# RMS weights folded into the up weights, a fixed token scale and a tanh read from PSUM in the last stage of an attention, mixture-of-experts and feed-forward kernel

## Chip, core and metric

The kernel runs on one core of one Trainium2 chip. The metric is the device time of one execution in microseconds (us). Matmuls run on TensorE (PE, with its weight loads PEld), elementwise work on VectorE (DVE), ScalarE (ACT) and GpSimd (POOL). Transfers are issued from the queues of SyncE (SP), ACT and POOL.

## The reference, cut to what matters

An attention with gates gives `x` of 3072 tokens by 320. A router sends each token to one of 8 experts (320 to 1024 to 320). The last stage, which the change is about, works on the result:

```
rms = sqrt(mean(x * x, axis=-1) + 1e-6)
xn  = x / rms * rms_g                      # rms_g: 320 weights
g   = xn @ w_gate                          # 320 x 1536
silu = g * (1 / (1 + exp(-g)))
out = (silu * (xn @ w_val)) @ w_out        # 1536 x 320
```

The weights arrive as float64. The kernel makes float32 of them on DVE (five integer steps, "narrowing") and then a pair of float16 values, high and rest. A product is three or so float16 matmuls: high by high, rest by high, high by rest.

## The kernel before

**Order.** The order on each engine and each queue is written out by hand. An engine takes its instructions strictly in that order. A DMA queue issues in order too, and an instruction that waits holds up all behind it. `route` sorts the tokens, `moe` runs the experts block by block, `moe_tail` ends it, and `ffn` is the last stage.

**Expert stage.** `moe` has a loop over 28 blocks `j` of 128 tokens. `gather(j)` fetches rows on POOL's queue, `xpose(j)` turns them on SP's queue into a tile `xt` (two buffers, so `xpose(2)` has to wait for the matmuls of `up(0)`), `up(j)` multiplies, and `down(j)`, two blocks later, multiplies with `W2A` and `W2B`. At its start POOL also has to finish two slices of `W2B` (L883, L884), behind `gather(2)` and `gather(3)`. `tick()` (L1160) works in the background on one weight job of the last stage: a load on SP, the five narrowing steps on DVE (L1265 to L1269), and a step that scales by `WSC` on ACT (L1290), takes the rest on DVE (L1296) and stores through POOL's queue. There are 24 jobs for the up weights (`UWS`) and four for the down weights (`DWS`), which come last. At blocks 23 to 26 (`FJ`) the first 512 tokens of the last stage are fetched, normalised and split (`fetch`, `norm1` to `norm4`).

**Last stage.** Six groups `n` of 512 tokens, each with 12 blocks `f` of 128 hidden units. `upf(n, f)` (L1492) does eight matmuls of 512 columns for the gate into the PSUM tile `pg` and eight for the value into `pv`. Both have one tag with four buffers, so block `f` writes over what block `f-2` held. Behind the matmuls: a product with `kvec` on DVE (L1502, it undoes the scale of each token), tanh on ACT (L1503), two products on DVE (`u`, L1510 and L1511), the float16 high part on ACT (L1516), the rest on POOL (L1517). `downf` of group `n-1` runs inside group `n`, behind block 9 (`DF`): four times 36 matmuls of 320 columns, an ACT copy with a scale for each token, and a scatter from POOL.

**Token scale.** `norm1` makes 1/rms, `norm2` multiplies by it and by the weights `G`, `peak` and `norm3` take a power of two for each token out of its largest value, `norm4` splits into float16, and `spread` and `undo` turn the inverse powers into the tile `kvec`, by four small matmuls (L1434) a group. For group 1 this runs beside group 0 (`beside`), from group 2 on inside `downf` (`stage`, with `DS`).

**Down weights.** Of 12 tiles, four come back from `DWS` and the other eight (`LJ`) are narrowed inside `upf`, by `wjob`: `more(1)` stands ahead of L1510 and another behind L1517, so two of the 40 narrowing steps go to a block, and the job's `rest` on POOL (L1486) frees the buffer for the next load `wload`. All of that has to be over before `downf(0)`.

Of the kernel before, what the change touches and what calls it, by code (L numbers as in the profile page):

```python
# [37 lines left out]
FJ = (23, 24, 25, 26)  # L38
LJ = 8
DF = 9  # L40
NS = (6, 8)
TS = ((0, 7),), ((1, 1), (2, 3), (3, 5))
DS = ((0, 1), (2,), (3, 4, 5, 6), (7,))
# [18 lines left out]
XSC = 2.0**-8  # L62
ORDER = (
# [12 lines left out]
class Net:  # L76
# [38 lines left out]
    def consts(self):  # L115
# [14 lines left out]
        self.NH = cp.tile([128, 4], F32, name="NH")  # L130
        self.zero = cp.tile([128, YC // 3], F32, name="zero3")
# [15 lines left out]
        self.DWS = dp.tile([NF, 128, 2 * DM], F16, name="DWS")  # L147
# [939 lines left out]
    def moe(self):  # L1087
# [70 lines left out]
        slot = [0]  # L1158

# [12 lines left out]
        for j in range(NJ):  # L1172
# [35 lines left out]
            if j == FJ[0]:  # L1208
                self.fetch(0, first=True)
            elif j == FJ[1]:  # L1210
                self.norm1(0)
                self.tokens(0)
            elif j == FJ[2]:
                for m in range(4):
                    self.norm2(0, m)
                self.norm3(0)
            elif j == FJ[3]:
                for m in range(4):
                    self.norm4(0, m)
# [52 lines left out]
    def ffn_jobs(self):  # L1272
        nc = self.nc
        jobs = []

        def job(src, n, fin):
            st = {}

            def load(t):
                t = st["t"] = t.bitcast(I32)  # L1280
                nc.sync.dma_start(t[:, 0 : 2 * n], src.bitcast(I32))

            def s1():
                st["v"], steps = self.narrow(st["t"], n)
                for step in steps:
                    step()

            def s2():
                of = st["t"][:, 0:320].bitcast(F16)
                nc.scalar.activation(of[:, 0:n], st["v"], AF.Copy, scale=WSC)  # L1290
                fin(st["v"], of, st["t"])

            return load, s1, s2

        def rest(out, v, hi):
            nc.vector.scalar_tensor_tensor(out=out, in0=v, scalar=WSC, in1=hi, op0=ALU.mult, op1=ALU.subtract)  # L1296

        def up(f, g):
            def fin(v, of, t):
                rest(of[:, 384:640], v[:, 0:256], of[:, 0:256])  # L1300
                rest(of[64:128, 256:384], v[64:128, 256:384], of[64:128, 256:384])
                nc.gpsimd.dma_start(self.UWS[f, :, g], of)  # L1302

            return job(self.i["wu"][f, g], 384, fin)

        def down(f):
            def fin(v, of, t):
                rest(of[:, DM : 2 * DM], v, of[:, 0:DM])
                nc.gpsimd.dma_start(self.DWS[f], of)

            return job(self.i["wo"][128 * f : 128 * f + 128], DM, fin)

        for f in range(NF):
            jobs += [up(f, 0), up(f, 1)]
        for f in range(NF - LJ):
            jobs.append(down(f))
        return jobs

    def fetch(self, n, first=False):
# [3 lines left out]
        for m in range(4):  # L1323
            i = 4 * n + m
            if first:
# [4 lines left out]
                if m == 3:  # L1330
                    self.G = t[:, DX : DX + DM]
                    u = self.stg()
                    self.idh0 = t[:, 3 * DX : 3 * DX + 64].bitcast(F16)
                    nc.gpsimd.tensor_copy(self.idh0, self.id)
                    X["xr"] = [
                        a.bitcast(F16).rearrange("p (s c) -> p s c", s=2)
                        for a in (t[:, 2 * DX : 3 * DX], u[:, 0:DX], u[:, DX : 2 * DX], u[:, 2 * DX : 3 * DX])
                    ]
                    nc.sync.dma_start(self.G, self.i["rg"].partition_broadcast(128))
# [8 lines left out]
    def norm1(self, n):  # L1348
# [5 lines left out]
        nc.vector.tensor_scalar(s[:, 1], s[:, 0], 1.0 / DM, 1e-6, ALU.mult, ALU.add)  # L1354
# [9 lines left out]
    def norm2(self, n, m, pool=False):  # L1364
        nc, X = self.nc, self.X[n]
        x, rs = X["yg"][m][:, 0:DM], X["rs"][:, m : m + 1]
        if pool:
            nc.scalar.activation(x, x, AF.Copy, scale=rs)  # L1368
            nc.gpsimd.tensor_tensor(x, x, self.G, ALU.mult)
            return  # L1370
        nc.vector.scalar_tensor_tensor(out=x, in0=x, scalar=rs, in1=self.G, op0=ALU.mult, op1=ALU.mult)
        self.peak(n, m)

    def peak(self, n, m):
        nc, X = self.nc, self.X[n]
        x = X["yg"][m][:, 0:DM]
        nc.vector.tensor_reduce(X["s"][:, 0, m : m + 1], x, AX.X, ALU.max, apply_absolute_value=True)  # L1377

    def norm3(self, n):

        nc, X = self.nc, self.X[n]
        mx, sc, ik, os = (X["s"][:, k] for k in (0, 3, 4, 5))
        mi = mx.bitcast(I32)
        nc.vector.tensor_scalar(mi, mi, 0x7F800000, None, ALU.bitwise_and)
        nc.vector.scalar_tensor_tensor(
            out=sc.bitcast(I32), in0=mi, scalar=float(27 << 23), in1=self.kmax.to_broadcast([128, 4]),
            op0=ALU.max, op1=ALU.subtract, reverse1=True,
        )
        nc.vector.tensor_scalar(ik.bitcast(I32), mi, float(27 << 23), float(-(1 << 23)), ALU.max, ALU.add)
        nc.vector.scalar_tensor_tensor(out=os, in0=ik, scalar=0.5 / WSC, in1=ik, op0=ALU.mult, op1=ALU.mult)  # L1390
        X["sc"], X["ik"], X["os"] = sc, ik, os

    def spread(self, n):
        nc, X = self.nc, self.X[n]
        X["ib"] = self.F.tile([128, 4, 128], BF, tag="ib", bufs=1, name="ib")
        nc.gpsimd.tensor_scalar(
            X["ib"], X["ik"].unsqueeze(2).to_broadcast([128, 4, 128]), 1.0 / WSC, 0.0, ALU.mult, ALU.add
        )

    def norm4(self, n, m, pool=False):  # L1400
        nc, X = self.nc, self.X[n]
        x, sc = X["yg"][m][:, 0:DM], X["sc"][:, m : m + 1]
# [3 lines left out]
        nc.scalar.activation(xr[:, 0, 0:DM], x, AF.Copy, scale=sc)  # L1406
        if pool:
            nc.scalar.activation(x, x, AF.Copy, scale=sc)
            nc.gpsimd.tensor_tensor(xr[:, 1, 0:DM], x, xr[:, 0, 0:DM], ALU.subtract)
        else:  # L1410
            nc.vector.scalar_tensor_tensor(
                out=xr[:, 1, 0:DM], in0=x, scalar=sc, in1=xr[:, 0, 0:DM], op0=ALU.mult, op1=ALU.subtract
# [16 lines left out]
    def undo(self, n):  # L1429

        nc, X = self.nc, self.X[n]
        ps = self.P.tile([128, 4, 128], F32, tag="px", bufs=2, name="ikp")
        for m in range(4):
            nc.tensor.matmul(ps[:, m], X["ib"][:, m], self.idb, start=True, stop=True)  # L1434
        X["kv"] = self.F.tile([128, 512], F32, tag="kvec", bufs=2, name="kvec")
        nc.scalar.activation(X["kv"], ps.rearrange("p m c -> p (m c)"), AF.Copy)

    def ffn(self):
# [11 lines left out]
        self.idb = one([128, 128], BF, "idb")  # L1450
        nc.gpsimd.tensor_copy(self.idb, self.id)
        self.spread(0)
        self.undo(0)
        for k in range(3):
            wload(NF - LJ + k)
        self.G = one([128, DM], F32, "G")
        nc.sync.dma_start(self.G, self.i["rg"].partition_broadcast(128))
# [4 lines left out]

        def dw(f):
            nc.sync.dma_start(DW[:, f].rearrange("p s c -> p (s c)"), self.DWS[f])
# [27 lines left out]
        def upf(n, f):  # L1492
# [9 lines left out]
            nc.vector.tensor_tensor(th, pg, self.X[n]["kv"], ALU.mult)  # L1502
            nc.scalar.activation(th, th, AF.Tanh, scale=0.5)  # L1503
            if n == 0 and f in NS:
                for m in (2 * NS.index(f), 2 * NS.index(f) + 1):
                    self.norm4(1, m, True)
# [5 lines left out]
                out=u, in0=u, scalar=1.0 / (WSC * WSC), in1=pv, op0=ALU.mult, op1=ALU.mult  # L1512
# [6 lines left out]
            more(0 if n == 0 and f in (4, 5) else 1)  # L1519

        def downf(n, beside):
            for m in range(4):
# [10 lines left out]
                nc.scalar.activation(o, ps[:, 0:DM], AF.Copy, scale=self.X[n]["os"][:, m : m + 1])  # L1533
# [8 lines left out]
        def stage(n, k):  # L1542
            if k == 0:
                norm1(n)
                self.tokens(n)
            elif k < 3:
                norm2(n, 2 * k - 2)
                norm2(n, 2 * k - 1)
                if k == 2:
                    self.norm3(n)  # L1550
                    self.spread(n)
            elif k < 7:
                self.norm4(n, k - 3)
                flip(n, k - 3)
            else:
                self.undo(n)

        def beside(f):
            if f == 1:
                norm1(1)  # L1560
                self.tokens(1)
            elif 2 <= f < 4:
                for m in (2 * f - 4, 2 * f - 3):
                    norm2(1, m, True)
            elif 4 <= f < 6:
                for m in (2 * f - 8, 2 * f - 7):
                    self.peak(1, m)
                if f == 5:
                    self.norm3(1)
                    self.spread(1)  # L1570
            elif f == 11:
                self.undo(1)
# [7 lines left out]
        for n in range(NB2):  # L1580
            nx = n + 1 < NB2
            for f in range(NF):
                upf(n, f)
                if n == 0:
                    beside(f)
                    if f == 1:
                        for k in range(NF - LJ):
                            dw(k)
# [12 lines left out]
def layout(inputs):  # L1601
# [52 lines left out]
    rg = f["moe2_rms_g"]  # L1654
# [32 lines left out]
```

## Time and profile before

| what | value |
|---|---|
| median of 3 runs | 839.25 us (832.34 to 839.45) |
| profiled execution | 837.3 us, its span 835.5 us |
| mean granted TensorE clock | 0.966 |
| busy in the span | PE 776.0 us (93%), DVE 511.7 (61%), POOL 381.6 (46%), ACT 350.3 (42%) |
| attention and routing | 0 to about 213 us |
| expert stage | about 213 to 457 us |
| last stage | 457 us to the end |

The span runs from the first to the last instruction. Busy shares are means over stages with different limits, so each stage is read by itself: from what PE waited for in it, and what the engines did in that time.

### The profile page before, as it was taken

To read this page: it belongs to the slowest core of one execution; us is meant where nothing else is said; L and a number is where in the kernel's file an instruction comes from. 1 tells how busy PE (TensorE), PEld (TensorE's weight loads), DVE (VectorE), ACT (ScalarE), POOL (GpSimd) and SP (SyncE) were. 2 spreads that over 40 slices of the span, in tenths; PEclk is the share of its full clock that TensorE was granted. 3 is DMA by queue.
4 is the path that set the end of the run, shared out by engine and by line. 5 is a ranking of instruction groups with operands and counts; after the bars stand their busy time and mean duration, and the time that the engine had idled before them with its cause. 6 is when DMAs were issued, how large, how long until landed. Compare 5 with 4: busy or idle time off the path is not lost. (4 is left out here: it accounts for less than half of the span.)

```text
span 835.5 us, 15652 instructions
## 1 busy us (share of the span) xinstructions
PE 776.0 (93%) x5312; PEld 489.9 (59%) x5312; DVE 511.7 (61%) x1026; ACT 350.3 (42%) x717; POOL 381.6 (46%) x454
## 2 busy tenths in 40 slices
PE   8999999998787797898988998999999999999996
PEld 8799988985344454454545443564564564554564
DVE  7678888886875666776341788745545546535310
ACT  4478877863322232223234554433423333333211
POOL 3456867762832332333523665454443443433221
PEclk9799999996999898999999999999999999999999
DMA  6587878846579999999987622030030040030000
GB/s 200 159 251 246 262 227 260 260 138 248 123 155 218 223 227 233 237 231 246 171 148 159 248 69 64 1 86 17 1 94 9 1 102 0 9 62 1 9 25 33
DMA packets 136023, 113.88 MB, mean 136 GB/s; under 512 B 107607, under 2 KB 115167, under 8 KB 135945
## 3 DMA queue, kind: packets, MB, share of 16 engines
q1 hardware_dynamic: 125001, 89.62, 42.5%
q0 software_dynamic: 6720, 18.42, 7.8%
q10 hardware_dynamic: 4224, 4.81, 1.9%
q8 instruction: 48, 0.79, 0.4%
q14 instruction: 30, 0.25, 0.1%
HBM read 69.88 MB, written 18.79 MB: 106 GB/s over the span
## 5 line engine op out<-in xcount | busy, mean ns | idle before, releaser
L1498 PE MATMUL gv<-XT,UW 128*128 128x512 f16 x1152 | 250.3, 379 | 4.3 <-DVE u L1510 4.3
L1498 PEld LDWEIGHTS <-UW 128*128 128x128 f16 x1152 | 112.5, 98 | 139.5 <-issue 5.2
L1517 POOL TENSOR_TENSOR h2l<-u,h2h 128x512 f16<-128x512 f32 x72 | 85.7, 1190 | 136.0 <-ACT h2h L1516 134.0
L1109 PE MATMUL ups<-W,xt 128*128 x448 | 112.3, 409 | 31.4 <-DMA xt<-xg 22.5
L1530 PE MATMUL do<-DW,h2h 128*128 128x320 f16 x576 | 119.0, 299 | 0.0
L1502 DVE TENSOR_TENSOR th<-gv,kvec 128x512 f32<-128x512 f32 x72 | 49.6, 689 | 90.8 <-PE gv L1498 76.4
L1109 PEld LDWEIGHTS <-xt 128*128 128x128 f16 x448 | 46.4, 104 | 90.9 <-DMA xt<-xg 34.9
L1516 ACT ACTIVATE h2h<-u 128x512 f16<-128x512 f32 x72 | 45.3, 629 | 108.7 <-DVE u L1511 108.7
L1530 PE MATMUL do<-DW,h2l 128*128 128x320 f16 x288 | 86.1, 299 | 0.0
L1139 PEld LDWEIGHTS <-hT 128*128 128x128 f16 x672 | 65.5, 98 | 33.1 <-issue 4.0
L1510 DVE SCALAR_TENSOR_TENSOR u<-th,gv 128x512 f32<-128x512 f32 x72 | 49.4, 686 | 46.3 <-ACT th L1503 27.7
L1114 DVE SCALAR_TENSOR_TENSOR h<-ups,h 128x512 f16<-128x512 f32 x56 | 37.7, 689 | 55.9 <-ACT h L1113 40.4
L1530 PEld LDWEIGHTS <-h2h 128*128 128x128 f16 x576 | 56.4, 98 | 22.2
L1503 ACT ACTIVATE th<-th 128x512 f32<-128x512 f32 x72 | 45.2, 628 | 48.6 <-DVE th L1502 48.6
L1113 ACT ACTIVATE h<-ups 128x512 f16<-128x512 f32 x56 | 32.5, 593 | 72.3 <-PE ups L1109 49.0
L1511 DVE SCALAR_TENSOR_TENSOR u<-u,gv 128x512 f32<-128x512 f32 x72 | 49.5, 687 | 7.5
L1139 PE MATMUL dps<-W2A,hT 128*128 x336 | 50.7, 299 | 3.1 <-ACTq L1226 2.2
L487 PE MATMUL S<-QK 104*128 104x128 f32 x384 | 52.3, 280 | 1.2 <-DMA QK<-in_pqk_dram 1.2
L543 PE MATMUL Y<-t,D 128*128 128x41 f32 x352 | 52.8, 254 | 0.0
L543 PEld LDWEIGHTS Y<-t,D 128*128 128x128 f32 x352 | 50.7, 197 | 3.4
L487 PEld LDWEIGHTS S<-QK 104*128 104x128 f32 x384 | 50.9, 197 | 2.7 <-issue 1.9
L1302 POOL DMA_DIRECT2D UWS<-stg x24 | 14.0, 582 | 83.0 <-ACT LG L1150 41.5
(289 smaller groups left out, 1273.5 us busy)
## 6 DMA issues: line engine op xcount, KB each, us to landing
t<-in_pk_dram SPq DMA_DIRECT2D x22, 484.0 KB
stg<-in_wu_dram SPq DMA_DIRECT2D x24, 384.0 KB
QK<-in_pqk_dram SPq DMA_DIRECT2D x48, 160.0 KB
stg<-in_w_dram SPq DMA_DIRECT2D x9, 640.0 KB
XD<-xr SPq DMA_DIRECT2D x23, 192.0 KB
YD<-LG ACTq DMA_DIRECT2D x26, 160.5 KB
stg<-in_w_dram SPq DMA_DIRECT2D x8, 512.0 KB
UWS<-stg POOLq DMA_DIRECT2D x24, 160.0 KB
```

What stands on the lines that cost most here:

```text
L487: nc.tensor.matmul(ps[:, i * L : (i + 1) * L], t["kz"][:, j, i], t["t1"][:, i], start=True, stop=True)
L543: nc.tensor.matmul(t["Y"][:, hp, 41 * hf : 41 * hf + 41], t["D"][hf][:, hp * L : (hp + 1) * L], t["vv"][:, 4 * hf + hp], start=False, stop ...
L1109: nc.tensor.matmul(ps, t["xt"][:, kx], self.W1[:, ds(o1 + (kw * F1 + f * 512), 512)], start=(n == 0), stop=(n == 7),)
L1139: nc.tensor.matmul(ps[:, 0:DM], hT[:, l, k % 4], r, start=(n == 0), stop=(n == 23))
L1498: nc.tensor.matmul(ps, UW[:, f, gv, kw], xt[:, :, 3 * hl + kx], start=(a == 0), stop=(a == 7))
L1502: nc.vector.tensor_tensor(th, pg, self.X[n]["kv"], ALU.mult)
L1503: nc.scalar.activation(th, th, AF.Tanh, scale=0.5)
L1510: nc.vector.scalar_tensor_tensor(out=u, in0=th, scalar=1.0, in1=pg, op0=ALU.add, op1=ALU.mult)
L1511: nc.vector.scalar_tensor_tensor(out=u, in0=u, scalar=1.0 / (WSC * WSC), in1=pv, op0=ALU.mult, op1=ALU.mult)
L1516: nc.scalar.activation(hh, u, AF.Copy)
L1517: nc.gpsimd.tensor_tensor(hl, u, hh, ALU.subtract)
L1530: nc.tensor.matmul(ps[:, 0:DM], l[:, s], DW[:, f, w], start=(a == 0), stop=(a == 3 * NF - 1))
```

## The change

The up weights are multiplied by the RMS weights while they are scaled (`gs`, one column for each 128 rows), so that tokens are multiplied by `XN`/rms only. `gs` is loaded through SP's queue and scaled on POOL at the start of `moe`. `peak`, `norm3`, `spread`, `undo` and `kvec` go, `norm2` now does what `norm4` did, tanh reads `pg` itself, and the inverse scales are constants. All 12 tiles of down weights are narrowed inside `upf` (`LJ` 12), three of 60 steps to a block, and the four `down` jobs, the store `DWS` and its four loads go.

```diff
-FJ = (23, 24, 25, 26)
-LJ = 8
+FJ = (23, 24, 25)
+LJ = 12
-NS = (6, 8)
+NS = (4, 6)
-DS = ((0, 1), (2,), (3, 4, 5, 6), (7,))
+DS = ((4,), (0, 1), (2, 3), ())
+XN = 2.0**11
...
+        nc.sync.dma_start(self.gs, self.i["rg"])
+        nc.gpsimd.tensor_scalar(self.gs, self.gs, WSC, 0.0, ALU.mult, ALU.add)
...
                 for m in range(4):
                     self.norm2(0, m)
-                self.norm3(0)
-            elif j == FJ[3]:
-                for m in range(4):
-                    self.norm4(0, m)
...
             def s2():
-                of = st["t"][:, 0:320].bitcast(F16)
-                nc.scalar.activation(of[:, 0:n], st["v"], AF.Copy, scale=WSC)
-                fin(st["v"], of, st["t"])
+                fin(st["v"], st["t"][:, 0:320].bitcast(F16))
...
-            def fin(v, of, t):
-                rest(of[:, 384:640], v[:, 0:256], of[:, 0:256])
-                rest(of[64:128, 256:384], v[64:128, 256:384], of[64:128, 256:384])
+            def fin(v, of):
+                for k in range(3):
+                    c = slice(128 * k, 128 * k + 128)
+                    nc.scalar.activation(of[:, c], v[:, c], AF.Copy, scale=self.gs[:, k : k + 1])
+                for k in range(3):
+                    c, p = slice(128 * k, 128 * k + 128), slice(64 if k == 2 else 0, 128)
+                    out = of[p, c] if k == 2 else of[:, 384 + 128 * k : 512 + 128 * k]
+                    nc.vector.scalar_tensor_tensor(
+                        out=out, in0=v[p, c], scalar=self.gs[p, k : k + 1], in1=of[p, c],
+                        op0=ALU.mult, op1=ALU.subtract,
+                    )
                 nc.gpsimd.dma_start(self.UWS[f, :, g], of)
...
-        for f in range(NF):
-            jobs += [up(f, 0), up(f, 1)]
-        for f in range(NF - LJ):
-            jobs.append(down(f))
-        return jobs
+        return [up(f, g) for f in range(NF) for g in range(2)]
...
-                    nc.sync.dma_start(self.G, self.i["rg"].partition_broadcast(128))
...
-        self.idb = one([128, 128], BF, "idb")
-        nc.gpsimd.tensor_copy(self.idb, self.id)
-        self.spread(0)
-        self.undo(0)
...
-        self.G = one([128, DM], F32, "G")
-        nc.sync.dma_start(self.G, self.i["rg"].partition_broadcast(128))
...
-            nc.vector.tensor_tensor(th, pg, self.X[n]["kv"], ALU.mult)
-            nc.scalar.activation(th, th, AF.Tanh, scale=0.5)
+            nc.scalar.activation(th, pg, AF.Tanh, scale=0.5 / (XN * WSC))
             if n == 0 and f in NS:
                 for m in (2 * NS.index(f), 2 * NS.index(f) + 1):
-                    self.norm4(1, m, True)
+                    norm2(1, m, True)
                     flip(1, m)
...
-            more(0 if n == 0 and f in (4, 5) else 1)
+            more(2)
...
-                nc.scalar.activation(o, ps[:, 0:DM], AF.Copy, scale=self.X[n]["os"][:, m : m + 1])
+                nc.scalar.activation(o, ps[:, 0:DM], AF.Copy, scale=0.5 / WSC)
...
         def stage(n, k):
-            if k == 0:
+            if k == 4:
                 norm1(n)
                 self.tokens(n)
...
-                self.undo(n)
-
-        def beside(f):
...
+                norm2(n, k)
+                flip(n, k)
...
-                if n == 0:
-                    beside(f)
-                    if f == 1:
-                        for k in range(NF - LJ):
-                            dw(k)
+                if n == 0 and f == 1:
+                    norm1(1)
+                    self.tokens(1)
```

## Rows read from the trace of the kernel before

**Rows 1.** Windows of the last stage: length, busy us (instructions) by engine, clock, DMA share, GB/s

```profile
core 0: us, PE busy (x) PEld busy (x) DVE busy (x) ACT busy (x) POOL busy (x), PEclk, DMA share, GB/s
457.15:538.30 81.15, 76.88 (x361) 34.70 (x359) 68.16 (x113) 40.97 (x81) 48.43 (x53) 1.00 0.34 103
510.51:538.30 27.79, 27.79 (x130) 12.62 (x130) 25.53 (x43) 13.10 (x24) 13.02 (x11) 1.00 0.04 12
558.00:619.00 61.00, 61.00 (x340) 32.92 (x339) 31.45 (x53) 21.32 (x41) 25.90 (x30) 1.00 0.15 37
```

**Rows 2.** The chain that ended last, group 1 to 2: start us, us, what

```profile
552.97 0.22 PE ikp L1434 x4
...
558.08 41.44 PE gv L1498 x192
```

**Rows 3.** PE's timeline, last stage: start, us, instruction [idle before <-releaser]

```profile
486.52 14.15 PE L1498 MATMUL gv<-XT,UW 128*128 128x512 f16 x64 [1.56 <-DVE u L1510]
...
510.51 27.79 PE L1498 MATMUL gv<-XT,UW 128*128 128x512 f16 x128 [2.71 <-DVE u L1510]
```

**Rows 4.** DVE's timeline, groups 0 and 1

```profile
468.24 0.17 DVE L1354 TENSOR_SCALAR nrm<-nrm 128x4 f32<-128x4 f32 x1 [2.27 <-ACT junk L1353]
...
504.74 3.67 DVE L1266 SCALAR_TENSOR_TENSOR wraw<-wraw 128x320 int32<-128x320 int32 x1
```

**Rows 5.** POOL's timeline beside that long DVE step

```profile
505.03 1.17 POOL L1517 TENSOR_TENSOR h2l<-u,h2h 128x512 f16<-128x512 f32 x1
506.14 0.80 POOL L1486 TENSOR_TENSOR DW<-wraw,DW 128x320 f16<-128x320 f32 x1
506.89 1.16 POOL L1517 TENSOR_TENSOR h2l<-u,h2h 128x512 f16<-128x512 f32 x1
```

**Rows 6.** Costliest groups of the page: count | busy, mean ns | idle before

```profile
L1502 DVE TENSOR_TENSOR th<-gv,kvec 128x512 f32<-128x512 f32 x72 | 49.6, 689 | 90.8 <-PE gv L1498 76.4
...
L1510 DVE SCALAR_TENSOR_TENSOR u<-th,gv 128x512 f32<-128x512 f32 x72 | 49.4, 686 | 46.3 <-ACT th L1503 27.7
```

**Rows 7.** Windows of the narrowing tile alone (DVE, ACT, POOL busy, instructions)

```profile
457.00:538.00 81.00, 26.80 (x40) 6.47 (x14) 5.88 (x7) 1.00 0.34 103
510.50:538.00 27.50, 10.43 (x17) 2.77 (x6) 2.45 (x3) 1.00 0.04 13
```

**Rows 8.** POOL's timeline where the expert stage starts: gathers 0 and 2, second slice

```profile
213.07 1.12 POOL L1069 DMA_INDIRECT xg<-XD,IDX  x1 [2.50 <-DVE IDX L972]
...
216.73 1.08 POOL L1069 DMA_INDIRECT xg<-XD,IDX  x1 [0.30 <-issue]
...
226.54 3.73 POOL L884 TENSOR_TENSOR W2B<-stg,W2B 128x1280 f16<-128x1280 f32 x1
```

**Rows 9.** SP queue's timeline in the expert stage

```profile
216.30 3.59 SPq L1077 DMA_TRANSPOSE xt<-xg  x2
219.98 0.53 SPq L876 DMA_DIRECT2D stg<-in_w_dram  x1
...
224.28 1.22 SPq L1077 DMA_TRANSPOSE xt<-xg  x1
...
376.35 1.23 SPq L1281 DMA_DIRECT2D stg<-in_wo_dram  x1
...
420.12 0.53 SPq L1339 DMA_DIRECT2D stg<-in_rg_dram  x1
```

**Rows 10.** SP queue's waits, 222 to 232 us: total, times, longest

```profile
SPq L1077 <- PE ups L1109: 3.6, 1, 3.6
```

**Rows 11.** PE's timeline in the expert stage

```profile
233.62 1.79 PE L1139 MATMUL dps<-W2B,hT 128*128 x12
...
237.97 3.61 PE L1109 MATMUL ups<-W,xt 128*128 x16 [1.62 <-DMA xt<-xg]
...
384.10 4.98 PE L1109 MATMUL ups<-W,xt 128*128 x16 [3.17 <-DMA xt<-xg]
...
425.12 4.95 PE L1109 MATMUL ups<-W,xt 128*128 x16 [3.20 <-DMA xt<-xg]
```

**Rows 12.** A background weight job's last steps on ACT and DVE, 375 to 378 us

```profile
376.37 0.52 ACT L1290 ACTIVATE stg<-stg 128x384 f16<-128x384 f32 x1 [1.98 <-DVE stg L1269]
...
376.93 0.73 DVE L1296 SCALAR_TENSOR_TENSOR stg<-stg 128x256 f16<-128x256 f32 x2 [0.59 <-ACT stg L1290]
```

More of the change, by code (lines that the diff above doesn't have):

```diff
@@ L130, in consts @@
         self.NH = cp.tile([128, 4], F32, name="NH")
+        self.gs = cp.tile([128, 3], F32, name="gs")
         self.zero = cp.tile([128, YC // 3], F32, name="zero3")
@@ L146, in consts @@
         self.UWS = dp.tile([NF, 128, 2, 5 * 128], F16, name="UWS")
-        self.DWS = dp.tile([NF, 128, 2 * DM], F16, name="DWS")
     def att_consts(self):
@@ L1288, in s2 @@
             def s2():
-                of = st["t"][:, 0:320].bitcast(F16)
-                nc.scalar.activation(of[:, 0:n], st["v"], AF.Copy, scale=WSC)
-                fin(st["v"], of, st["t"])
+                fin(st["v"], st["t"][:, 0:320].bitcast(F16))
             return load, s1, s2
-        def rest(out, v, hi):
-            nc.vector.scalar_tensor_tensor(out=out, in0=v, scalar=WSC, in1=hi, op0=ALU.mult, op1=ALU.subtract)
         def up(f, g):
-            def fin(v, of, t):
-                rest(of[:, 384:640], v[:, 0:256], of[:, 0:256])
-                rest(of[64:128, 256:384], v[64:128, 256:384], of[64:128, 256:384])
+            def fin(v, of):
[9 more added lines that the diff above has]
+                    )
                 nc.gpsimd.dma_start(self.UWS[f, :, g], of)
             return job(self.i["wu"][f, g], 384, fin)
[L1306 to L1311, printed above, removed]
-        for f in range(NF):
-            jobs += [up(f, 0), up(f, 1)]
-        for f in range(NF - LJ):
-            jobs.append(down(f))
-        return jobs
+        return [up(f, g) for f in range(NF) for g in range(2)]
     def fetch(self, n, first=False):
@@ L1330, in fetch @@
                 if m == 3:
-                    self.G = t[:, DX : DX + DM]
                     u = self.stg()
@@ L1353, in norm1 @@
             nc.scalar.activation(junk[:, 0:DM], X["yg"][m][:, 0:DM], AF.Square, accum_out=s[:, 0, m : m + 1])
-        nc.vector.tensor_scalar(s[:, 1], s[:, 0], 1.0 / DM, 1e-6, ALU.mult, ALU.add)
+        k = 1.0 / (XN * XN)
+        nc.vector.tensor_scalar(s[:, 1], s[:, 0], k / DM, 1e-6 * k, ALU.mult, ALU.add)
         nc.gpsimd.tensor_tensor(s[:, 2], s[:, 1], self.NH, ALU.pow)
@@ L1366, in norm2 @@
         x, rs = X["yg"][m][:, 0:DM], X["rs"][:, m : m + 1]
[L1367 to L1402, printed above, removed]
         if len(X["xr"]) == m:
@@ L1405, in norm4 @@
         xr = X["xr"][m]
-        nc.scalar.activation(xr[:, 0, 0:DM], x, AF.Copy, scale=sc)
+        nc.scalar.activation(xr[:, 0, 0:DM], x, AF.Copy, scale=rs)
         if pool:
-            nc.scalar.activation(x, x, AF.Copy, scale=sc)
+            nc.scalar.activation(x, x, AF.Copy, scale=rs)
             nc.gpsimd.tensor_tensor(xr[:, 1, 0:DM], x, xr[:, 0, 0:DM], ALU.subtract)
@@ L1411, in norm4 @@
             nc.vector.scalar_tensor_tensor(
-                out=xr[:, 1, 0:DM], in0=x, scalar=sc, in1=xr[:, 0, 0:DM], op0=ALU.mult, op1=ALU.subtract
+                out=xr[:, 1, 0:DM], in0=x, scalar=rs, in1=xr[:, 0, 0:DM], op0=ALU.mult, op1=ALU.subtract
             )
@@ L1427, in flip @@
         )
[L1429 to L1436, printed above, removed]
     def ffn(self):
@@ L1461, in ffn @@
         fetch, norm1, norm2, flip = self.fetch, self.norm1, self.norm2, self.flip
-        def dw(f):
-            nc.sync.dma_start(DW[:, f].rearrange("p s c -> p (s c)"), self.DWS[f])
         fill = []
@@ L1511, in upf @@
             nc.vector.scalar_tensor_tensor(
-                out=u, in0=u, scalar=1.0 / (WSC * WSC), in1=pv, op0=ALU.mult, op1=ALU.mult
+                out=u, in0=u, scalar=1.0 / (XN * WSC) ** 2, in1=pv, op0=ALU.mult, op1=ALU.mult
             )
@@ L1542, in stage @@
         def stage(n, k):
-            if k == 0:
+            if k == 4:
                 norm1(n)
                 self.tokens(n)
[L1546 to L1554, printed above, removed]
-            else:
-                self.undo(n)
-        def beside(f):
-            if f == 1:
[L1560 to L1572, printed above, removed]
+            else:
+                norm2(n, k)
+                flip(n, k)
         fetch(1)
@@ L1583, in ffn @@
                 upf(n, f)
-                if n == 0:
-                    beside(f)
-                    if f == 1:
-                        for k in range(NF - LJ):
-                            dw(k)
+                if n == 0 and f == 1:
+                    norm1(1)
+                    self.tokens(1)
                 while rests and 5 * (len(rests) - 1) >= len(fill):
@@ L1653, in layout @@
     gate = lambda a: a[:, perm].reshape(32, S)
-    rg = f["moe2_rms_g"]
+    g = f["moe2_rms_g"]
+    rg = np.stack([g[0:128], g[128:256], np.tile(g[256:DM], 2)], axis=1)
     w1 = f["moe_w1"][:, 0:256].reshape(NE, 2, 128, F1).transpose(0, 2, 1, 3)
```

## The prediction, made blind

> **What bounds the kernel now.** I read the windows by stage first. From 558 us on, a group takes 61.00 us and PE is busy for all of it [rows 1]. There the chain is nothing but matmuls: 41.44 us for 12 blocks of `upf`, or 3.45 us a block, and between the `do` matmuls the four `kvec` ones, 0.22 us [rows 2]. What the change takes from DVE, ACT and POOL in groups 2 to 5 is therefore worth nothing; the cover is PE itself. Only a removed matmul counts.
>
> Next, the start of the last stage. From 457.15 to 538.30 us PE did 22 blocks, which need 22 x 3.45 = 76.0 us, and took 81.15 [rows 1]: 5.2 us lost, 0.2 of it `kvec`. PE's timeline puts the large pieces at 485 and 508 us, 1.56 and 2.71 us, both ended by L1510 [rows 3]: DVE had not read `pg` in time, and the buffer two blocks on was not free. DVE was late because it stood 2.27 us for the first norm of group 1 and because one narrowing step took 3.67 us [rows 4] while POOL ran three instructions without a gap [rows 5].
>
> Third, PE's waits in the expert stage. Before that stage settles, PE waits for turned rows (1.62 us at 236 us); later it waits for them where weight loads crowd the DMAs, 3.17 us ahead of 384.10 and 3.20 us ahead of 425.12 [rows 11]. Sixteen matmuls then took 4.98 and 4.95 us; after the short wait they took 3.61 [rows 11].
>
> **The change, part by part**, against the profiled execution's 837.3 us (1.95 below the median of 839.25).
>
> *`kvec` matmuls.* Six times 0.22 us on PE [rows 2]: **-1.3 us**. Their ACT copies, `spread` and the products of L1502 lie beside PE.
>
> *DVE in the first 20 blocks.* Per block L1502 goes, 0.69 us, as do the peaks and scales of group 1; two products of 0.69 stay [rows 6], and two narrowing steps become three. A step cost 26.80/40 = 0.67 us in this stretch, and 10.43/17 = 0.61 in its last third [rows 7]. So a block asks 1.38 + 3 x 0.61 = 3.21 us of DVE, against 3.45 on PE. The nearest comparison is that last third of before: DVE busy 25.53 of 27.79 us (3.17 a block), and PE without a gap [rows 1]. The disturbances stay: the 2.27 us wait and a `fetch` that heaps up POOL's work. But tanh no longer waits for DVE, and a product may be late by about a block, 3.45 us, before PE feels it. Either disturbance alone stays below that; both add up only if the 36 us between them give nothing back (ten blocks x 0.24 us do). I keep 0.5 us of the 5.0: **-4.5** (bounds: -5.0, PE cannot gain more than it lost; and 0, if the stalls stay; the loss side is the second rival).
> POOL gets four more `rest` steps and loses four products with `G`, so I leave the 0.61. The 12 jobs take 60 steps and end in block 7 of group 1, two blocks before `downf(0)` wants them. The four loads of `DWS`, at 466 us, go with them.
>
> *The end of the expert stage.* Four jobs go: their loads (320 KB each, the first at 376.35 us [rows 9], 1.8 us ahead of the turned rows that came late), 20 narrowing steps, four stores and loads of 160 KB. PE works through this stretch but for the one wait, so at most the wait and the slowed matmuls come back: 3.17 + (4.98 - 3.61) = 4.5 us [rows 11]. The load was one of two large transfers ahead, so I take half the wait, 1.6 us; the rest then resembles the 1.62 us wait after which matmuls ran in 3.61, so 1.4 more: -3.0. The broadcast of `G`, one of several transfers ahead of 425.12 us, is issued at 420.12 [rows 9]: by the same sum at most 4.5, of which I take 0.7, a quarter of the wait with nothing for the clock. **-3.7** (bounds 0 and -9.1). That `norm3` and the fourth step at block 26 go lies off PE's path and gets nothing.
>
> *The start of the expert stage: a wait is added.* POOL must scale `gs` ahead of `gather(2)`, and `gs` is issued on SP behind two transposes and a 640 KB load that went out at 219.98 to 220.5 us [rows 9]. The nearest landing is that of `gather(0)`, issued until 214.2 and turned from 216.30 on [rows 8, 9]: 2.1 us. With issue and the load ahead I put `gs` at 223.9 us. `gather(2)`, then at 216.73 [rows 8], slips by 7.2 us, and with it on POOL `gather(3)`, two slices of `W2B`, `gather(4)` and all behind. Who waits? `xpose(2)` started at 224.28 after standing 3.6 us for PE [rows 9, 10], so it had slack: the rows now land at 223.9 + 1.1 + 2.1 = 227.1, 2.8 us late. The slice that ended at 230.27 [rows 8] ends at 237.5, and the `W2B` half of `down(0)`, started at 233.62 [rows 11], slips by 3.9. Then PE had 1.62 us of waiting [rows 11] into which this falls. **+2.0** (bounds 0, and +7.2 if all of it reaches PE).
>
> *Up jobs.* 24 times one ACT copy of 384 columns, 0.52 us, becomes three of 128, and two DVE rests of 0.73 us together become three [rows 12]. The second rest can run beside the third copy, so the chain hardly grows; DVE has cover in a stage in which PE waits for transfers. 0 (up to +3 if a third of a us reaches PE in every third job; below 0 is excluded, as nothing is removed).
>
> Sum: -1.3 - 4.5 - 3.7 + 2.0 = -7.5, so **829.8 us**, 9.4 below the median.
>
> **Rivals.**
> 1. *The gains of the last stage, without the rest:* the `gs` wait reaches PE whole and the waits at 384 and 425 us stay, since other transfers crowd there too. 837.3 - 1.3 - 4.5 + 7.2 = 838.7. For it: every gather behind POOL's wait is late. Against: the 3.6 and 1.62 us of slack. Chance 0.18.
> 2. *Slower: the narrowing steps bind the first 20 blocks.* DVE is the bound once a step costs more than (3.45 - 1.38)/3 = 0.69 us; before it was 0.67 over the whole stretch. In the long step POOL's three instructions ended at 508.05, the step at 508.41 [rows 4, 5]: it stood until POOL paused. If each step meets half of a POOL instruction of 1.16 us on top of some 0.42, it costs 1.0, a block 4.38, and 20 blocks lose 18.6 - 3.5 = 15.1 instead of 5.0: 837.3 - 1.3 - 3.7 + 2.0 + 10.1 = 844.4. If each meets a whole one, 1.58, a block is 6.1 and the kernel 880. Against: POOL was busy 48.43 of 81.15 us [rows 1], and still the mean was 0.67. Chance 0.15, most of it above 847.6.
> The Trainium skill, "SBUF — State Buffer", section "Who interferes with whom", says that a DVE instruction with two SBUF inputs and a GpSimd one that reads SBUF block each other for a whole instruction. The 3.67 us step agrees; by that rule alone this rival would be the forecast.
> 3. *The stalls of the last stage stay* because the first norm and the `fetch` cause them, not the load on DVE. 837.3 - 1.3 - 3.7 + 2.0 = 834.3. Chance 0.15.
> 4. *All waits go:* 837.3 - 1.3 - 5.0 - 9.1 = 821.9, with the start's delay absorbed. Chance 0.12.
>
> **How the numbers follow.** The forecast has 0.40 and its own range, 826 to 834. About 1% (8.4 us) can be told from no change, so faster ends at 830.9 and slower begins at 847.6. Faster: 0.29 of the forecast, 0.12 of rival 4, a hundredth elsewhere: 0.42. Slower: 0.10 of rival 2 and 0.02 for rivals 1 and 3 with dear up jobs: 0.12. The same: 0.46. The range from 822 to 841 leaves out most of rival 2 and the edge of rival 4.
>
> **What would show it.** PE between its first `gv` matmul and the first `do`: 76 to 77 us if the DVE sum holds, over 81 if rival 2 does, with L1510 as the releaser. The mean of a narrowing step: 0.6 or above 0.7. POOL's idle time ahead of `gather(2)`: 7 us; `up(3)`, at 237.97 before, about 2 us later. The waits near 384 and 425 us: near 1.6 and 2.5. Groups 2 to 5: 0.22 us shorter each and otherwise alike. The forecast is wrong if the expert stage, which hangs on how transfers meet, moves by more than 4 us for a reason that is none of these.

## The result, and the profile after

Over 20 runs of each, the changed kernel's median is 829.87 us against 836.36 us: ratio 0.9917, 95% interval [0.9889, 0.9945], that is 4.6 to 9.3 us less. Beside the experiments it was run again: 826.22 us, 0.9997 [0.9963, 1.0031]. The two intervals do not meet. So the gain is clear of the noise in one set of runs and about nothing in the other, and its size is known only as between 0 and 1%. Over the four sets of runs the kernel before alone took 836.36, 833.86, 827.58 and 831.54 us, so ratios are compared within a set as far as that can be done. The ratios leave out runs more than 1.5% above the fastest of their kernel; with all runs the two ratios of medians are 0.992 and 0.998. The profiled execution took 826.0 us, its span 824.1.

The span is 11.4 us shorter than that of before, but 3.8 us of this lie ahead of any edit: the last warm-up matmuls, which end the routing, start at 208.52 us and not at 212.28. I therefore cut both traces at three places: the start of those matmuls, the first gate matmul of the last stage, the first down matmul.

| stretch, us | before | after | by the prediction |
|---|---|---|---|
| expert stage: warm-up to first gate matmul | 244.87 | 240.98 | -1.9, one `kvec` in it |
| last stage up to the first down matmul | 80.98 | 78.66 | -4.7, one `kvec` in it |
| from there to the end of the span | 297.37 | 295.94 | -0.9, four `kvec` in it |

PE's timeline ahead of `up(2)` before, and of the changed kernel, where the expert stage starts and later, and in the last stage (as in [rows 3, 11]; lines moved, L1109 is now L1110, L1498 is L1435):

```profile
228.54 3.61 PE L1109 MATMUL ups<-W,xt 128*128 x16 [0.83 <-DMA xt<-xg]
```
```profile
229.53 5.18 PE L1110 MATMUL ups<-W,xt 128*128 x16 [6.32 <-DMA xt<-xg]
...
239.71 3.61 PE L1110 MATMUL ups<-W,xt 128*128 x16 [1.63 <-DMA xt<-xg]
...
367.79 3.61 PE L1110 MATMUL ups<-W,xt 128*128 x16 [2.97 <-DVE stg L1265]
...
411.27 0.38 PE L1110 MATMUL ups<-W,xt 128*128 x1 [1.91 <-issue]
...
474.14 7.12 PE L1435 MATMUL gv<-XT,UW 128*128 128x512 f16 x32 [0.15 <-DVE u L1446]
481.74 17.43 PE L1435 MATMUL gv<-XT,UW 128*128 128x512 f16 x80 [0.47 <-DVE u L1446]
500.54 19.80 PE L1435 MATMUL gv<-XT,UW 128*128 128x512 f16 x91 [1.37 <-DVE u L1446]
```

The first line after shows the price of the new wait: 6.32 us ahead of `up(2)`, where 0.83 stood before, and matmuls that took 5.18 us instead of 3.61: the granted clock was 0.69 of 2.4 GHz over them, so they ran in part at 1.2 GHz, and 1.00 over the sixteen at 239.71, behind a wait of 1.63. The waits at 384 and 425 us [rows 11] are gone, with smaller ones at 368 and 411. In the last stage the stalls behind DVE fell from 4.3 to 2.0 us.

POOL's timeline at the start of the expert stage and SP's issue of the weights (answers to [rows 8, 9]):

```profile
221.13 1.12 POOL L1161 TENSOR_SCALAR gs<-gs 128x3 f32<-128x3 f32 x1 [8.46 <-DMA gs<-in_rg_dram]
222.40 2.21 POOL L1070 DMA_INDIRECT xg<-XD,IDX  x1 [0.16 <-POOL gs L1161]
```
```profile
216.81 0.42 SPq L1160 DMA_DIRECT2D gs<-in_rg_dram  x1
```

The scaling of `gs` could start 3.9 us after the issue had ended, behind the 640 KB load, and took 1.12 us. `gather(2)` starts 13.9 us after the warm-up, against 4.5: a slip of 9.4 us.

Windows of the last stage (as [rows 1]) and of the narrowing tile in it (as [rows 7]), DVE's longest step and what POOL did beside it (as [rows 4, 5]):

```profile
449.66:528.32 78.66, 76.66 (x355) 34.45 (x353) 64.35 (x103) 40.32 (x83) 47.72 (x52) 1.00 0.37 112
...
449.66:528.32 78.66, 38.35 (x60) 11.23 (x24) 10.72 (x12) 1.00 0.37 112
```
```profile
495.95 3.94 DVE L1265 SCALAR_TENSOR_TENSOR wraw<-wraw 128x320 int32<-128x320 int32 x1
```
```profile
495.55 0.95 POOL L1331 DMA_INDIRECT yg<-YD,RSLOT  x1 [0.30 <-issue]
496.52 2.27 POOL L1453 TENSOR_TENSOR h2l<-u,h2h 128x512 f16<-128x512 f32 x2
498.75 0.78 POOL L1423 TENSOR_TENSOR DW<-wraw,DW 128x320 f16<-128x320 f32 x1
```

Sixty steps at 38.35/60 = 0.64 us, DVE busy 64.35 us instead of 68.16, and the one step that waits until POOL has worked off the fetch is still there: POOL ends at 499.53, the step at 499.89, and the stall ahead of 500.54 follows. A group is now 61.00 us from gate matmul to gate matmul, 41.44 + 19.56 with nothing else between; before, it was 61.22 (from 558.08 to 619.30 us), 0.22 of it `kvec` [rows 2]. (The 61.00 us of before in [rows 1] are the length of the window that was asked for, not that of a group.) The chain after has no `kvec` piece:

```profile
528.32 19.56 PE do L1466 x144
547.88 41.44 PE gv L1435 x192
```

### The profile page after: what moved, and what is told of

Its sections match the earlier page's. It is cut to its first block, busy times and chain, and to the rows that moved or that the text cites. A ratio compares the mean times of both kernels' runs of the same rounds, so it can differ in the third digit from the quotient of the medians.

```text
span 824.1 us, 15461 instructions
## 1 busy us (share of the span) xinstructions
PE 764.9 (93%) x5288; PEld 482.5 (59%) x5288; DVE 444.9 (54%) x906; ACT 352.3 (43%) x759; POOL 371.2 (45%) x444
## 5 line engine op out<-in xcount | busy, mean ns | idle before, releaser
L1435 PE MATMUL gv<-XT,UW 128*128 128x512 f16 x1152 | 250.3, 379 | 2.0 <-DVE u L1446 2.0
L1435 PEld LDWEIGHTS <-UW 128*128 128x128 f16 x1152 | 112.7, 98 | 137.7 <-issue 3.3
L1110 PE MATMUL ups<-W,xt 128*128 x448 | 108.7, 398 | 33.0 <-DMA xt<-xg 20.4
L1110 PEld LDWEIGHTS <-xt 128*128 128x128 f16 x448 | 45.4, 101 | 90.3 <-DMA xt<-xg 32.9
L1471 POOL DMA_INDIRECT out_dram<-os,TKN x24 | 24.1, 1002 | 71.9 <-ACT os L1469 61.8
L1439 ACT ACTIVATE th<-gv 128x512 f32<-128x512 f32 x72 | 42.6, 592 | 26.6 <-PE gv L1435 26.6
L488 PEld LDWEIGHTS S<-QK 104*128 104x128 f32 x384 | 49.1, 191 | 5.0 <-issue 4.2
L1296 ACT ACTIVATE stg<-stg,gs 128x128 f16<-128x128 f32 x72 | 23.6, 390 | 65.0 <-DVE stg L1268 46.3
```

The lines of the kernel that those rows point to most:

```text
L488: nc.tensor.matmul(ps[:, i * L : (i + 1) * L], t["kz"][:, j, i], t["t1"][:, i], start=True, stop=True)
L1110: nc.tensor.matmul(ps, t["xt"][:, kx], self.W1[:, ds(o1 + (kw * F1 + f * 512), 512)], start=(n == 0), stop=(n == 7),)
L1435: nc.tensor.matmul(ps, UW[:, f, gv, kw], xt[:, :, 3 * hl + kx], start=(a == 0), stop=(a == 7))
L1439: nc.scalar.activation(th, pg, AF.Tanh, scale=0.5 / (XN * WSC))
```

## Experiments

The theory: the three terms of the prediction, each as large as it was put. The rivals: the start's wait costs more (or is taken up later), the four jobs were hidden, the last stage's stalls come from single events. The runs came in three groups of four, each on a chip of its own with its own runs of before; only the second group has the changed kernel beside it. Traces are single executions; the times are what counts where both exist.

**Weights early.** POOL's wait is taken out: load on POOL's queue at the start, scaling in the routing stage.

```diff
-        nc.sync.dma_start(self.gs, self.i["rg"])              # in moe
-        nc.gpsimd.tensor_scalar(self.gs, self.gs, WSC, 0.0, ALU.mult, ALU.add)
+        nc.gpsimd.dma_start(self.gs, i["rg"])                 # in const_fill
+        nc.gpsimd.tensor_scalar(self.gs, self.gs, WSC, 0.0, ALU.mult, ALU.add)   # in route, behind rb
```

> The changed kernel with the RMS weights loaded on POOL's queue at the very start and scaled on POOL in the routing stage, behind the products that make the gather lists, where POOL stood idle 2.50 us; nothing else differs, so POOL has no wait ahead of gather(2). Theory A (the wait reaches PE and is carried to the end): PE's idle time ahead of up(2), 6.32 us in the changed kernel, falls to about the 0.83 of before, its 16 matmuls take 3.61 instead of 5.18 us, up(3) starts 4 to 5.5 us earlier counted from the warm-up matmuls, and the time is 825 to 826.5 us (ratio 0.987 to 0.989). Theory B (the expert stage is set by its transfers and takes the delay up later): up(3) is earlier by as much, but the first matmul of the last stage is not, and the time is 829 to 830.5.

Measured: ratio 0.9887 [0.9828, 0.9945]; `up(3)` 26.5 us after the warm-up (31.19 in the changed kernel), expert stage 234.31 us. POOL's timeline:

```profile
207.07 0.50 POOL L962 TENSOR_SCALAR gs<-gs 128x3 f32<-128x3 f32 x1
...
213.25 1.08 POOL L1072 DMA_INDIRECT xg<-XD,IDX  x1 [0.30 <-issue]
```

`gather(2)` is back at 4.2 us after the warm-up, and `up(2)` behind 0.77 us of waiting. The delay at `up(3)` is the wait's. The ratio and the expert stage are those of Theory A, but the interval takes in Theory B's time too (0.991 to 0.993 of before), so how much of the delay arrives at the end it does not say.

**The scale part alone** (`LJ` 8, the `down` jobs, `DWS` and its loads back):

```diff
-LJ = 12
+LJ = 8
-        return [up(f, g) for f in range(NF) for g in range(2)]
+        return [up(f, g) for f in range(NF) for g in range(2)] + [down(f) for f in range(NF - LJ)]
```

> The changed kernel with four down weights narrowed in the background of the expert stage again (LJ 8, their stores and loads back), so of the change only the folding of the RMS weights, the fixed scale and tanh from PSUM are left; three narrowing steps to a block, 40 in all. Theory A (the end of the expert stage gives back 3.7 us or more once the four jobs are gone): 833.5 to 835.5, with a wait of PE for turned rows again where the four jobs run, and the last stage's stretch to the first down matmul as in the changed kernel or up to 1 us shorter. Theory B (the jobs were hidden in the expert stage): 829 to 830.5.

Measured: 0.9986 [0.9947, 1.0026]. Folding, fixed scale and tanh from PSUM, with the wait they bring, gain nothing that shows. That is the ratio of Theory A (0.997 to 0.999), but with the changed kernel itself at 0.9917 and 0.9997 it does not prove it. In its trace, a long execution, the last stage took 79.35 us to the first down matmul, no less than with 60 steps, although only 40 are left.

**The move alone** (kernel before, `LJ` 12):

```diff
-LJ = 8
+LJ = 12
-            more(0 if n == 0 and f in (4, 5) else 1)
+            more(1 if n == 0 and f in (4, 5) else 2)
```

> The kernel before with all 12 down weights narrowed in the last stage (LJ 12, three steps to a block, two in blocks 4 and 5), token scales, kvec products and the RMS product kept. Theory A (DVE's load per block decides): a block asks 3 x 0.69 + 3 x 0.64 = 3.99 us of DVE against 3.45 of PE, so 20 blocks fall behind by 10.8 us, of which a block's 3.45 is free, and with the peaks of group 1 the stretch from the first gate matmul to the first down matmul takes 87 to 90 us instead of 81.15; with 3.7 us given back by the expert stage the time is 838 to 842. Theory B (the stalls come from single events, the first norm and the fetch, and not from the load): the stretch stays at 80 to 82 us and the time is 832 to 834.

Measured: 0.9987 [0.9952, 1.0023]. The last stage up to the first down matmul took 84.97 us, PE waiting for L1510 six times:

```profile
PE gv L1498 <- DVE u L1510: 5.3, 6, 2.5
```

Three steps beside three products are too much, so the load does count, though the stretch grew by 4.0 us and not by 6 to 9, and the time fits neither theory. The steps cost 34.58/60 = 0.58 us there, less than the 0.64 I had taken. The expert stage was 235.23 us, 9.6 shorter than before, in one execution. Neither half of the change shows a gain by itself. That the fold makes the room on DVE that the move needs is seen in the stretch: 84.97 us with three products, 78.15 to 79.90 with two and the same 60 steps. That the whole is faster than either half is not shown, as the whole was not run on this chip.

**Fetch late.** Group 2 is fetched behind block 7 of group 1:

```diff
-                if f == 9 and n + 2 < NB2:
-                    fetch(n + 2)
+                if (n == 1 and f == 7) or (n and f == 9 and n + 2 < NB2):
+                    fetch(2 if f == 7 else n + 2)
```

> The changed kernel with the fetch of group 2 issued behind block 7 of group 1, when the narrowing is over, instead of behind block 9 of group 0. Theory A (the one long narrowing step, 3.94 us, which waits until POOL has worked off what the fetch heaped up, makes the stall of 1.37 us): no narrowing step above 1.6 us, the stretch from the first gate matmul to the first down matmul takes 76.5 to 77.5 us instead of 78.66, time 828 to 829. Theory B (DVE is behind anyway): the stretch stays above 78 and the time at 829.9. If the fetch comes too late for the norm of group 2, PE waits behind down(0) and the time rises by 1 to 5 us.

Measured: 0.9934 [0.9899, 0.9968]; the stretch 78.08 us, the narrowing tile 35.62 us on DVE instead of 38.35. The long step is gone (the longest took 1.45 us), as Theory A has it, but the stretch and the time of this run are nearer to Theory B. Six traces, below, decide for a part of Theory A.

**The changed kernel again**, as a yardstick for the next three.

> The changed kernel itself, as the yardstick for the three beside it on the same chip and for a second trace of the same code. Ratio 0.9917 as measured first, within 0.988 to 0.996; warm-up matmuls to first gate matmul 239 to 243 us (240.98 and 240.45 in two traces of this code), first gate to first down matmul 78 to 79 us.

Measured: 0.9997 [0.9963, 1.0031], outside what was expected. Its trace is like the first: expert stage 242.71, then 79.90, just above the 79 expected.

**Both moves together:**

> Both moves together on the changed kernel: RMS weights loaded at the start and scaled in the routing stage, fetch of group 2 behind block 7 of group 1. Theory A (the wait for the weights is carried through the expert stage): 3.5 us or more earlier at up(3), warm-up to first gate matmul 234 to 237 us, and with 0.6 us from the fetch the time is 4 to 7 us below the changed kernel beside it (ratio 0.984 to 0.988). Theory B (absorbed): within 1.5 us of the changed kernel.

Measured: 0.9895 [0.9857, 0.9934], 1.0% (some 8 us) below the changed kernel beside it, more than either theory has. `up(3)` came 2.3 us earlier than beside it, not 3.5, and the expert stage took 230.23 us. The last stage took 76.60 us to the first down matmul, with PE's stalls down to one:

```profile
PE gv L1435 <- DVE u L1446: 0.5, 1, 0.5
```

Over all traces with two products and 60 steps that stretch is 78.66, 79.90, 78.78, 78.15 and 79.12 us with the fetch of the change, and 78.08, 76.60, 77.15, 77.13, 77.08 and 77.14 with the late one. The means are 78.9 and 77.2: the event is worth 1.7 us, and rival 3 was right about that much. PE's timelines show it, too: some 51 us after the first gate matmul PE stalls for 1.37 to 1.39 us in all six traces with the fetch of the change (the scale part alone included), and in none of the six with the late one.

**Four loads, nothing else**, at the end of the background jobs:

```diff
+        for f in range(4):
+            load = job(self.i["wo"][128 * f : 128 * f + 128], DM, None)[0]
+            jobs.append((load, lambda: None, lambda: None))
```

> The changed kernel with the four loads of 320 KB put back at the end of the background jobs, into staging buffers that nothing reads: transfers alone, without narrowing, scaling, storing. Theory A (the removed loads are what the end of the expert stage gave back): from the down matmuls of block 17 to those of block 25 it takes 63 to 65 us, as with the jobs, instead of about 58, and the time is 4 to 6 us above the changed kernel beside it. Theory B (the work of DVE, ACT and POOL and the stores, or none of it, made the difference): that stretch stays below 60 us and the time within 1.5 us of the changed kernel.

Measured: 1.0011 [0.9976, 1.0046], against 0.9997 beside it; blocks 17 to 25 took 55.4 us. So Theory B: the loads, to which the prediction put the wait at 384 us, are not by themselves what the end of the expert stage gave back.

**Two more waits** of the same kind ahead of `gather(2)`:

```diff
+        for _ in range(2):
+            nc.gpsimd.dma_start(self.gx, self.i["rg"])
+            nc.gpsimd.tensor_scalar(self.gx, self.gx, WSC, 0.0, ALU.mult, ALU.add)
```

> The changed kernel with two more loads of the RMS weights on POOL's queue behind the first scaling, each followed by a scaling that waits for it, ahead of gather(2): POOL's wait there grows from about 8 us by 6 to 8 us more. Theory A (every us of that wait beyond the slack of about 3 us reaches the end): the stretch from the warm-up to the first gate matmul grows by 6 to 8 us and so does the time. Theory B (the expert stage takes it up): up(2) is later by as much, the first gate matmul by less than 2 us, and the time stays within 1.5 us of the changed kernel beside it.

Measured: 0.9976 [0.9945, 1.0008]. PE's timeline of this run:

```profile
235.57 5.16 PE L1111 MATMUL ups<-W,xt 128*128 x16 [10.08 <-DMA xt<-xg]
```

`up(2)` started 24.7 us after the warm-up, 5.7 later than in the changed kernel beside it (18.97). But the `W2B` matmuls of `down(3)` came at 53.3 us against 54.6: a wait of PE that the yardstick had at that place, 4.18 us ahead of 256.81, was not there. The expert stage took 237.08. So Theory B: what is added to the start need not reach the end. Why that later wait was gone is not shown; by the profile it ended with a step of a background job on DVE.

**Both moves again**, as a yardstick on another chip.

> The kernel with both moves (RMS weights early, fetch of group 2 late) once more, as the yardstick of the three beside it. Ratio 0.9895 as measured first, within 0.985 to 0.994; from the warm-up to the first gate matmul 230 to 235 us; from the first gate matmul to the first down matmul 76.5 to 78.1 us.

Measured: 0.9898 [0.9853, 0.9943]. PE's timeline of its two ends of the expert stage, and those of the same code in the earlier run (211.06 and 441.29):

```profile
206.90 4.49 PE L916 MATMUL warm<-W,cst 128*128 128x512 bf16 x20
...
448.53 3.83 PE L1435 MATMUL gv<-XT,UW 128*128 128x512 f16 x17
```

241.63 us here, outside the 230 to 235 expected, and 230.23 there. One execution's expert stage differs from another's by up to 11 us with nothing changed in the code, so no single trace of it sizes an edit of a few us.

**The four jobs added** to that kernel, in full, with the results unread:

```diff
-        return [up(f, g) for f in range(NF) for g in range(2)]
+        return [up(f, g) for f in range(NF) for g in range(2)] + [down(f) for f in range(4)]
```

> The same with the four background jobs of the expert stage put back in full (load, five narrowing steps, scale, rest, store), their stored result never read, all 12 tiles still narrowed in the last stage; so the jobs alone are added. Theory A (the removed jobs gave back 4 to 6 us): from block 17's to block 25's down matmuls 63 us or more instead of 54 to 60, time 4 to 6 us above the yardstick (ratio 0.994 to 0.997). Theory B (they were hidden, and traces differ there by chance): that stretch as in the yardstick, the time within 1.5 us of it.

Measured: 0.9928 [0.9895, 0.9962], against 0.9898 beside it: +0.3%, 2.5 us, with intervals that overlap. Blocks 17 to 25 took 61.31 us, against 57.41 beside it. Both lie between the two theories.

**The four jobs without transfers:**

```diff
+                if n == DM:
+                    return nc.gpsimd.memset(t[:, 0 : 2 * n], 0)
...
-                nc.gpsimd.dma_start(self.DWS[f], of)
```

> The same with the four jobs, but each load replaced by a fill on POOL and no store: the DVE and ACT work alone. Theory A1 (the narrowing steps, queued on DVE ahead of the relu rests, delay the expert stage): as the kernel with the four jobs, 3 us or more above the yardstick. Theory A2 (the transfers of loads and stores together do it): within 1.5 us of the yardstick.

Measured: 0.9873 [0.9827, 0.9920]. By the times DVE's and ACT's part of the jobs costs nothing, but an interval of half a per cent to each side can hardly tell 3 us from none. Its trace, of the longest of its six executions, says otherwise: blocks 17 to 25 took 64.86 us, as Theory A1 has it, with two waits of PE, 3.35 us (by the profile for a step of a background job on DVE) and 3.55 us (for turned rows). Over all traces this stretch took 65.82, 63.83, 61.31 and 64.86 us in the four with the jobs' work on DVE and ACT, and 53.9 to 62.4 us in the ten without. So whether that work costs anything stays open.

**No fold in the up jobs:**

```diff
-                for k in range(3):
-                    nc.scalar.activation(of[:, c], v[:, c], AF.Copy, scale=self.gs[:, k : k + 1])
...
+                nc.scalar.activation(of[:, 0:384], v, AF.Copy, scale=WSC)
...
```

> The yardstick with the up weights scaled as in the kernel before (one ACT copy and two DVE rests by a constant, 24 times), which leaves the RMS weights out of the result. Theory A (the two more ACT and one more DVE instruction of a job are hidden, as the prediction took it): within 1.5 us of the yardstick. Theory B (a third of a us a job reaches PE): 3 to 7 us below the yardstick, ratio 0.981 to 0.986.

Measured: 0.9895 [0.9840, 0.9950], against 0.9898. No cost of the 24 jobs' two more ACT and one more DVE instruction shows, though a copy of 128 columns took 390 ns where a third of 522 was to be hoped for; the interval reaches down to the edge of Theory B.

## Why the prediction came out

It said 829.8 us, and the runs gave 829.87 and, the second time, no difference. The agreement to 0.1 us is luck. The sum was counted down from a profiled execution of 837.3 us, where the median of 20 runs is 836.36; of its terms one came out as put, one half as large, one larger, and one cannot be sized by the runs.

- *`kvec` matmuls, -1.3:* right. From the first down matmul to the end all traces with the fixed scale gave 295.9 to 296.1 us, against 297.37; the group is 0.22 us shorter. Of these 1.4 us, 0.9 are the four `kvec` pieces. The other 0.5 lie behind the last matmul and are mostly not the change's: the move alone, which keeps the token scale, took 296.92 us, and 5.83 us behind its last matmul, where before took 6.29 and the changed kernel 5.73.
- *DVE in the first 20 blocks, -4.5:* the load was right (0.64 us a step against 0.61, and a stretch below 81 us, so rival 2 is out), the size was not: -2.1, without the `kvec` piece. The step that failed is the slack, "a product may be late by about a block, 3.45 us, before PE feels it", and with it "Either disturbance alone stays below that". By PE's timeline a gate buffer is needed again 5.2 us after the gate matmuls that filled it (half a block and a block: 1.73 + 3.45). In the changed kernel the gate products of blocks 3 to 11 ended 3.9 to 5.7 us after their gate matmuls, and those of blocks 14 to 21 3.9 to 4.9; in the run of the scale part alone, once its 40 steps were over, 1.48. So while there are steps to do, most of the slack is used up. The long step at 496 us met a lag of 3.9 us and made 6.5 of it, and PE stalled 1.37 us. The late fetch takes that stall away.
- *Tanh:* "tanh no longer waits for DVE", in the same term, did not hold either. Tanh stands on ACT behind the float16 copy of the block before, which waits for DVE, and DVE's next product waits for tanh:

```profile
488.81 0.63 ACT L1452 ACTIVATE h2h<-u 128x512 f16<-128x512 f32 x1 [2.52 <-DVE u L1447]
```
```profile
491.11 0.69 DVE L1446 SCALAR_TENSOR_TENSOR u<-th,gv 128x512 f32<-128x512 f32 x1 [1.34 <-ACT th L1439]
```

- *The start, +2.0:* the mechanism was right, in its place and with its slack. Mis-sized was the landing of `gs` (slip 9.4 us, in three other traces 8.1 to 8.6, and not 7.2), and the slower clock behind the longer wait was left out. `up(3)` started 31.2, 28.5, 28.9 and 28.8 us after the warm-up in four traces with the wait, and after 25.7 to 27.2 us in eight without it: 2.7 us between the means (29.4 and 26.6), not 2.0. How much reaches the end is not settled: taking the wait out, with the fetch moved as well, gained 1.0% on one chip; adding to it cost nothing.
- *The end of the expert stage, -3.7:* this is a size that the times allow (the four jobs, added, cost 2.5 us, with intervals that overlap). But its cause as I put it, the 320 KB load ahead of the late rows, fell: four such loads alone cost nothing, neither in time nor in the trace. What is left is the work on DVE and ACT, for which the traces speak and the times do not, and the stores through POOL's queue, or load and store together, which were not tried. The cause stays open. Sorted by what they hold, the expert stages took 244 to 245 us in the three traces with the jobs' work and no wait, 239 to 243 in four with the wait and no such work, and 230 to 242 in five with neither (250.74 with both, in a long execution; 237.08 with two more waits). By these single executions, on several chips, both this term and the start's would be larger than they were put, and cancel in part.
- *Up jobs, 0:* no cost shows, and the +3 that was its bound is hardly excluded.
- *Rival 1* (start whole, end nothing) is not excluded: in the first trace `up(3)` was 5.5 us later than before, and the second measurement, 0.9997, is where it would have put the time.
- *The rule of the Trainium skill* ("SBUF — State Buffer", "Who interferes with whom") agrees with the longest step here, 3.94 us until POOL's three instructions were over. The two SBUF inputs of which that rule speaks are not the whole, as steps with one SBUF operand (L1267) were held up beside POOL too, for up to 1.30 us instead of 0.32. It did not decide: 33 of the 60 steps met a POOL instruction that computes, but only 13 took more than 0.9 us.

The kernel with the two moves beats the changed one where both ran side by side, 0.9895 against 0.9997, and was 0.9898 of before on another chip.

## What to carry to other kernels

Before an instruction is put on an in-order engine, ask for its operand's landing and what is queued behind it: three columns of weights held a gather up for 8 to 9 us, and an issue some 190 us earlier cost nothing that shows. Work moved onto a busy engine needs room there: the three steps took the stretch to 84.97 us beside three products and to 79 beside two. Slack counts only from where the engine stands when it is disturbed, and an engine that is busy for most of each block may have used it up. Where a stage hangs on transfers, size an edit by medians of many runs and by stretches that repeat (from the first down matmul on, all traces with the fixed scale agreed to 0.2 us), not by one trace.

## What the hardware showed beyond what was expected

- A DVE step between two SBUF operands got no turn between POOL instructions that follow each other without a gap: 3.94 and 3.67 us instead of 0.48, for three computing POOL instructions each time, while products with a PSUM operand kept 0.67 to 0.69 us throughout.
- A load of 12 bytes a partition let its waiter start 3.3 to 4.3 us after its issue had ended, in six traces, on SP's queue behind a 640 KB load; on POOL's queue, with nothing of that kind ahead, it was 1.47 and 1.44 us. Whether the load ahead or the queue makes the difference no run separates.
- The expert stage of the same code took 230.23 and 241.63 us in two executions, on two chips.
